# One written order for all units in place of a planner, in a linear-attention and expert-layer kernel

## The chip, the cores and the metric

The kernel runs on one core of one Trainium2 chip. A core has five engines that run side by side and wait for each other by semaphores: PE (matmuls and transposes; its weight loads are listed as PEld), DVE (elementwise work), ACT (functions of one argument, copies with a scale), POOL (here: small copies and the loads of expert weights) and SP (here: all other loads and stores). Each engine works through its own instructions strictly in the order in which the program wrote them. The metric is the device time of one execution in microseconds, as the median of several runs.

## The reference

```python
# attention, for each of 8 batches and 8 heads, 576 tokens, head size 64
phi  = where(x > 0, x, exp(x) - 1) + 1
kv   = einsum('bhsd,bhse->bhde', phi(k), v)    # 64 x 64 for each head
z    = sum over tokens of phi(k)
x    = (phi(q) @ kv) / (phi(q) @ z + 1e-6)      # -> 8 x 576 x 512
# expert layer: 8 experts, 512 -> 1024 -> 512, one expert for each token
logits = x @ w_gate;  local = sigmoid(x @ w_local)
e      = argmax(logits) where s == 0 or local < 0.5, else the expert of the token before
out    = softmax(logits)[e] * (relu(x @ w1[e]) @ w2[e])
```

With these inputs every token of a batch uses the expert of its first token. The kernel computes with one expert for each batch and counts tokens for which this doesn't hold; only where there is one does a second, general program run (it does not run here).

## The kernel before

**Units.** The work is cut into 803 units, each a handful of instructions on one engine (some are only placeholders for a landing). A unit is a call `op(name, engine, length, rank, needs, function, takes, gives)` (lines 721 to 887). With `a` the batch (0 to 7), `n = 2a + j` a half of its heads, `h` a half of its tokens, they are:

- loads on SP: Lk, Lv, Lq (576 KB each, for every n), the stores ST, and HOLD, which stands in front of the loads of n = 4 and later until the first expert weights have landed; there are 4 buffers for k, 2 for q, 3 for v;
- E and E2 on ACT (exp and relu of k or q, lines 359 and 365), P on DVE (their sum, lines 387 and 394), VC (v copied beside ones, line 406), CL (the clamp of the first two k, line 379);
- K on PE (phi(k) times v, line 415: 72 matmuls with 72 weight loads), KC on DVE (its copy, line 420);
- Q and QL on PE (transposes of phi(q), lines 426 and 440), QC and QLC on ACT (their copies, lines 432 and 446);
- N and NL on PE (phi(q) times kv, lines 467 and 486), D and DL on DVE (the division, lines 452 to 455);
- X and XL on PE (transposes of x, lines 501 and 513), XC and XLC on DVE (their copies, lines 506 and 517);
- R on PE (the logits, lines 528 and 534), RC, PK, BK on DVE (copy, choice of the expert and of a weight slot, bookkeeping; lines 539 to 572), W on POOL (the load of the expert's w1 and w2, left out where the expert is in a slot already; lines 586 to 598), CW on DVE (copy of a slot into the current weights, lines 608 and 612);
- S1, S2, S3 on DVE, ACT, DVE (softmax value of the expert, lines 622 to 643);
- H on PE (8 for each batch, x times w1, line 650), HC on ACT (relu, line 657), O0 and O on PE (5 outputs for each batch, lines 669 and 673), OC on ACT (times the softmax value, lines 683 and 685).

The expert part of batch a runs on PE as H a 0 to H a 7, O0 a, O a 0 to O a 4. Units of the attention of later batches are written between these. K, N and NL work on 64 x 64 tiles of the array, the others mostly on the whole array.

**Planner.** `in_order` (lines 25 to 156) plays a schedule: each engine is free at some time, each unit has a length, a rank and needs; at each event each free engine takes the ready unit with the lowest rank, waits for a soon-ready one of lower rank, and so on. Ranks are nudged by hand-kept numbers, one table for each batch (`LATER`, lines 216 to 225). For PE it counts instructions in blocks and lets a block arrive some time after the one before it was entered:

```python
            wait += max(0.0, have - at)
            new.append(max(at, have) + (par["fetch"] if now < par["busy"] else par["fetch2"]))
```

with `"block": 256, "count": 62, "fetch": 5.6, "fetch2": 3.6` and the number of PE instructions of a unit as `instr` gives it (lines 205 to 213). What leaves the planner is only the order; the waits at run time are semaphores between the instructions.

**PSUM.** There are four slots of two banks. A unit that takes a slot gets the one that is free the earliest in the plan; at most 2 are held by units of kind "a" (attention, logits) and 3 by units of kind "m" (H, O). A unit then waits for the unit that gave the slot back.

**Products of zeros.** `work(n)` (line 895) writes n matmuls of a tile of zeros (128 x 512) ahead of a unit, into a slot of their own that is held from FILL to FILLED: 21 ahead of QL 0, 8 ahead of K 0, 2 ahead of NL 0, 4 ahead of XL 0, 2 ahead of R 0 0.

Of the kernel before, what the change touches and what calls it, by code (L numbers as in the profile page):

```python
# [22 lines left out]


def in_order(ops, slots, cap, rings, par):

    near, patience, hop = par["near"], par["patience"], par["hop"]
    n = len(ops)
    at_ = {op[0]: i for i, op in enumerate(ops)}
    users = [[] for _ in ops]
    miss = [0] * n
    for i, op in enumerate(ops):
        miss[i] = len(op[4])
        for d in op[4]:
            users[at_[d]].append(i)
    engines = list(dict.fromkeys(op[1] for op in ops))  # L40
    free_at = {e: 0.0 for e in engines}
    ready = {e: [] for e in engines}
    due = [0.0] * n
    slot = [0.0] * len(slots)
    held = {c: 0 for c in cap}
    left = {r: [0.0] * k for r, k in rings.items()}
    got = {}
    begun, done, order = {}, {}, []
    for i in range(n):
        if not miss[i]:  # L50
            ready[ops[i][1]].append(i)
    last_q = False
    now, todo, later = 0.0, n, set()

    def place(kind, k):

        if held[kind] == cap[kind]:
            return None, None
        best = min(((max(slot[i], now), slots[i], i) for i in range(len(slots))
                    if slots[i] >= k and slot[i] is not None), default=None)  # L60
        return (None, None) if best is None else (best[2], slot[best[2]])

    block = par["block"]
    count, there = par["count"], [0.0, 0.0]

    def stalled(name, length):

        k, wait, t = par["instr"](name), 0.0, now
        b = (count - 1) // block
        new = []  # L70
        while (b + 1) * block < count + k:
            b += 1
            at = now + wait + length * (b * block - count) / k
            have = new[-1] if b >= len(there) else there[b]
            wait += max(0.0, have - at)
            new.append(max(at, have) + (par["fetch"] if now < par["busy"] else par["fetch2"]))
        return k, wait, new

    events = [0.0]
    while todo:  # L80
        if not events:
            raise AssertionError([ops[i][0] for e in engines for i in ready[e]][:20])
        now = heapq.heappop(events)
        while events and events[0] <= now:
            heapq.heappop(events)
        for e in engines:
            if free_at[e] > now:
                continue
            best, soon = None, []
            for i in ready[e]:  # L90
                name, _, length, rank, needs, takes, gives = ops[i]
                at, where = due[i], None
                if takes:
                    if takes[1]:
                        where, t = place(*takes)
                        if where is None:
                            continue
                    else:
                        if not left[takes[0]]:
                            continue  # L100
                        t = min(left[takes[0]])
                    at = max(at, t)
                if e == "PE":
                    if last_q and par["quarter"](name):
                        rank -= par["cont"]
                    if at <= now:
                        rank += par["stall"] * stalled(name, length)[1]
                if at > now:
                    heapq.heappush(events, at)
                    soon.append((rank, at))  # L110
                elif best is None or rank < best[0]:
                    best = (rank, i, where)
            if not best:
                continue
            rank, i, where = best
            name, _, length, _, needs, takes, gives = ops[i]
            if isinstance(length, tuple):
                length = length[free_at["WQ"] > now + 1]
            if any(r < rank - near and t < now + (0.9 if r < -60 else patience) * length for r, t in soon):
                continue  # L120
            if e == "PE":
                q = par["quarter"](name)
                if q and not last_q:
                    length = length + par["switch"]
                last_q = q
                k, wait, new = stalled(name, length)
                count += k
                there += new
                length += wait
            ready[e].remove(i)  # L130
            order.append(name)
            begun[name] = now
            end = free_at[e] = done[name] = now + length
            todo -= 1
            heapq.heappush(events, end)
            if takes:
                if takes[1]:
                    slot[where] = None
                    held[takes[0]] += 1
                    got[name] = where  # L140
                else:
                    left[takes[0]].remove(min(left[takes[0]]))
            if gives:
                t = ops[at_[gives]][5]
                if t[1]:
                    slot[got[gives]] = end + hop
                    held[t[0]] -= 1
                else:
                    left[t[0]].append(end + hop)
            for u in users[i]:  # L150
                miss[u] -= 1
                due[u] = max(due[u], end + (0.0 if ops[u][1] == e else hop))
                if not miss[u]:
                    ready[ops[u][1]].append(u)
                    heapq.heappush(events, due[u])
    return order, begun, done, got
# [3 lines left out]
def kernel(  # L160
# [12 lines left out]
    P = 128  # L173
    B, H, S, Dh = q.shape
# [9 lines left out]
    NJ = 2  # L184
# [11 lines left out]
    CAP = {"a": 2, "m": 3}  # L196

    def quarter(name):

        return name[0] in ("K", "N", "NL") or name[0] == "R" and name[2] == 0 or name[0] == "O" and name[2] == NC - 1  # L200


    fills = {("QL", 0): 21, ("K", 0): 8, ("NL", 0): 2, ("XL", 0): 4, ("R", 0, 0): 2}

    def instr(name):

        t = name[0]
        n = {"K": 8 * C * NJ, "N": 64, "NL": 32, "Q": 16, "QL": 4, "X": 16, "XL": 4, "H": 16, "O0": 14, "TOT": 4}.get(t, 0)
        if t == "R":
            n = 32 if name[2] else 16  # L210
        if t == "O":
            n = (2, 16, 16, 16, 32)[name[2]]
        return n + 2 * fills.get(name, 0)


    LATER = [
# [8 lines left out]
    ]  # L225

    PAR = {"near": 3.0, "patience": 0.2, "hop": 0.2, "cont": 20.0, "switch": 0.2, "quarter": quarter,
           "instr": instr, "block": 256, "count": 62, "fetch": 5.6, "fetch2": 3.6, "busy": 125, "stall": 10.0}

# [8 lines left out]
    with ExitStack() as main:  # L238
# [482 lines left out]
        def op(name, eng, length, rank, needs, fn, takes=None, gives=None):  # L721
            ops.append((name, eng, length, rank + later(name), [d for d in needs if d], takes, gives))
            run[name] = fn

        def later(name):

            kind = name[0]
            if kind == "lat":
                return 0
# [415 lines left out]
```

## Time and profile before

| | |
|---|---|
| median of 3 runs | 228.78 us (227.97 to 231.41) |
| the profiled execution | 228.7 us |
| its span, first to last instruction | 226.8 us |
| granted TensorE clock | 0.997 |
| busy PE / DVE / ACT | 208.7 / 153.9 / 155.3 us |
| first H on PE (H 0 0) | 26.87 us |
| first O0 on PE (O0 0) | 42.51 us |
| last matmul ends | 220.57 us |

The page gives busy time by engine and the chain of work that ended last. The view of waits names, for each wait, the engine and line that waited, then the one it waited for, the total in us, how often, and the longest. The timeline of an engine has the start and duration in us of a run of like instructions, and in brackets the idle time before it with what ended it. "issue" there is time in which the engine waited for nothing that the profile shows.

### The profile page before, as it was taken

The page shows a single profiled execution, that of the slowest core. Times are in us where ns is not written, and L with a number is a line of the kernel's source. Part 1 is how long each engine was busy: PE and PEld are TensorE (multiplying, and loading weights), DVE is VectorE, ACT ScalarE, POOL GpSimd, SP SyncE. Part 2 cuts the span into 40 slices and gives each one's busy share as a digit, 9 for nine tenths or more (in the row PEclk, how much of TensorE's full clock was granted, in tenths as well). Part 3 has the DMA queues.
Part 4 walks back from the last instruction along what each step waited for, and adds up shares of the span by engine and source line. Part 5 has one row for each costly group of instructions (what it writes and reads, how often), then busy time and mean ns, then how long its engine had stood idle before and what let it go on. Part 6 is the DMA issues. An engine that isn't in the chain of part 4 may idle for free.

```text
span 226.8 us, 8581 instructions
## 1 busy us (share of the span) xinstructions
PE 208.7 (92%) x3705; PEld 149.1 (66%) x3719; DVE 153.9 (68%) x428; ACT 155.3 (68%) x226; POOL 13.1 (6%) x41
## 2 busy tenths in 40 slices
PE   7996799799999999999987996999999999999990
PEld 2465688458876678865775584865887678648540
DVE  1868986798999896866949975793783857412300
ACT  3698877899999949697797765935736355546440
POOL 4004000010001000020000000110000003000000
PEclk9999999999999999999999999999999999999998
DMA  6999999585788698989992656089700018985032
GB/s 209 382 347 353 203 271 399 205 312 203 224 259 299 200 359 254 389 143 258 307 313 87 228 218 214 3 145 192 246 7 0 4 46 198 204 136 208 3 143 78
DMA packets 24142, 46.78 MB, mean 206 GB/s; under 512 B 2834, under 2 KB 8978, under 8 KB 23202
## 3 DMA queue, kind: packets, MB, share of 16 engines
q1 hardware_dynamic: 16914, 37.58, 46.8%
q0 software_dynamic: 6832, 8.45, 22.7%
q8 instruction: 31, 0.51, 0.9%
q10 hardware_dynamic: 352, 0.13, 0.2%
q14 instruction: 13, 0.11, 0.1%
HBM read 61.88 MB, written 9.44 MB: 314 GB/s over the span
## 4 chain that ended last, share of the span: by engine, by line
PE 52%; DMA 9%; DVE 9%; issue 3%; ACT 0%; DVEq 0%
PE yps L669 18%; PE hps L650 17%; DMA w2s<-in_moe_w_dram 9%; PE nps L467 4%; PE kvps L415 3%; PE tq L426 3%; PE yps L673 3%; PE tx L501 2%; DVE xb L455 2%; DVE fq L394 1%; DVE w2cur L612 1%; DVE xT L506 1%; PE lps L534 1%; DVE rec L454 1%; DVE w1cur L612 1%
## 5 line engine op out<-in xcount | busy, mean ns | idle before, releaser
L650 PE MATMUL hps<-xT,w1cur 128*128 128x288 bf16 x512 | 69.2, 286 | 2.6 <-issue 1.9
L657 ACT ACTIVATE hT<-hps 128x576 bf16<-128x576 f32 x64 | 41.3, 652 | 30.8 <-PE hps L650 30.8
L669 PE MATMUL yps<-w2cur,hT 128*128 128x512 bf16 x243 | 58.2, 379 | 2.5 <-DVE w2cur L612 1.8
L650 PEld LDWEIGHTS <-w1cur 128*128 128x128 bf16 x512 | 48.2, 98 | 15.2 <-issue 2.4
L669 PEld LDWEIGHTS <-hT 128*128 128x128 bf16 x256 | 24.3, 98 | 27.4 <-issue 2.0
L683 ACT ACTIVATE yo<-yps,pr 128x512 f32<-128x512 f32 x32 | 22.0, 690 | 22.3 <-PE yps L669 20.9
L455 DVE TENSOR_TENSOR xb<-nps,rec 128x512 bf16<-128x512 f32 x32 | 22.1, 691 | 1.1
L394 DVE SCALAR_TENSOR_TENSOR fq<-fq,qraw 128x576 f32<-128x576 f32 (+1 forms) x32 | 22.5, 739 | 0.0
L467 PE MATMUL nps<-kv,qT 64*64 64x65 f32 x1024 | 20.4, 221 | 2.3 <-ACT qT L432 2.1
L467 PEld LDWEIGHTS nps<-kv,qT 64*64 64x64 f32 x1024 | 17.4, 134 | 5.6 <-ACT qT L432 2.8
L359 ACT ACTIVATE ek<-kraw 128x1152 f32<-128x1152 f32 x16 | 18.5, 1158 | 3.3 <-DMA kraw<-in_k_dram 2.1
L432 ACT COPY qT<-tq 128x512 f32<-128x512 f32 x32 | 18.3, 639 | 2.0 <-PE tq L426 2.0
L415 PE MATMUL kvps<-vone,kraw 64*64 64x65 f32 x1152 | 19.6, 219 | 0.0
L359 ACT ACTIVATE fq<-qraw 128x1152 f32<-128x1152 f32 (+1 forms) x16 | 18.4, 1153 | 1.4 <-DMA qraw<-in_q_dram 1.4
L415 PEld LDWEIGHTS kvps<-vone,kraw 64*64 64x64 f32 x1152 | 18.1, 134 | 1.8 <-issue 0.4
L387 DVE SCALAR_TENSOR_TENSOR kraw<-ek,kraw 128x1152 f32<-128x1152 f32 x14 | 18.9, 1348 | 0.0
L365 ACT ACTIVATE qraw<-qraw 128x1152 f32<-128x1152 f32 (+1 forms) x16 | 18.4, 1151 | 0.3
L426 PE MATMUL tq<-ident,fq 128*128 128x128 f32 x128 | 16.9, 275 | 0.3 <-DVE lt_all L539 0.2
L365 ACT ACTIVATE kraw<-kraw 128x1152 f32<-128x1152 f32 x14 | 16.1, 1163 | 0.2
L426 PEld LDWEIGHTS tq<-ident,fq 128*128 128x128 f32 x128 | 14.2, 141 | 1.5 <-DVE lt_all L539 0.5
L612 DVE COPY w2cur<-w2s 128x4096 bf16 x7 | 8.5, 1220 | 7.7 <-PE yps L673 4.6
L506 DVE COPY xT<-tx 128x1024 bf16<-128x1024 bf16 x16 | 10.8, 683 | 3.4 <-PE tx L501 3.2
(93 smaller groups left out, 187.0 us busy)
## 6 DMA issues: line engine op xcount, KB each, us to landing
kraw<-in_k_dram SPq DMA_DIRECT2D x16, 576.0 KB, 8.1
vraw<-in_v_dram SPq DMA_DIRECT2D x16, 576.0 KB, 6.5
qraw<-in_q_dram SPq DMA_DIRECT2D x14, 576.0 KB, 5.9
w1s<-in_moe_w_dram POOLq DMA_DIRECT2D x7, 1024.0 KB, 9.3
w2s<-in_moe_w_dram POOLq DMA_DIRECT2D x7, 1024.0 KB, 17.3
out_dram<-yo SPq DMA_DIRECT2D x14, 512.0 KB, 4.9
qraw<-in_q_dram SPq DMA_DIRECT2D x2, 512.0 KB, 8.6
w1cur<-in_moe_w_dram POOLq DMA_DIRECT2D x2, 512.0 KB, 7.7
```

The source lines that it names most:

```text
L359: nc.scalar.activation(e[:, :, c0:c1, :], raw_, Act.Exp)
L365: nc.scalar.activation(raw_, raw_, Act.Relu)
L387: nc.vector.scalar_tensor_tensor(r, e, 1.0, r, Alu.min, Alu.add)
L394: nc.vector.scalar_tensor_tensor(e[:, g], e[:, g], 1.0, r[:, g], Alu.min, Alu.add)
L415: nc.tensor.matmul(ps[g * PH:(g + 1) * PH, t, :W], lhsT=f[h, g, c, :], rhs=vo[h, g, c, :], start=(c == 0), stop=(c == C - 1))
L426: nc.tensor.transpose(ps[:, r, i * P:(i + 1) * P], ex_[n, "q"][:, 1 + i + (NC - 1) * r, :, :], identity=ident)
L455: nc.vector.tensor_tensor(dst, ps[:, :, :, :Dh].rearrange("p g (i t) e -> p g i t e", t=2), rec.rearrange("p g (i t o) -> p g i t o", t=2, ...
L467: nc.tensor.matmul(ps[o * PH:(o + 1) * PH, g, (il * 2 + t) * W:(il * 2 + t + 1) * W], lhsT=qT[n][g * PH:(g + 1) * PH, t, i * P + o * PH:i ...
L650: nc.tensor.matmul(ps[:, u, :HS], lhsT=w1b[:, kk, m * P:(m + 1) * P], rhs=xT[b][:, kk, u * HS:(u + 1) * HS], start=(kk == 0), stop=(kk == ...
L657: nc.scalar.activation(hT[b][:, m, :].rearrange("p (u s) -> p u s", u=2), open_.pop(("H", b, m))[:, :, :HS], Act.Relu)
L669: nc.tensor.matmul(ps, lhsT=hT[b][:, m, i * P:(i + 1) * P], rhs=w2b[:, m, :], start=(m == 0), stop=(m == FK - 1))
L683: nc.scalar.activation(ym[:, i, :], ps, Act.Copy, scale=pr[:, i:i + 1])
```

## The change

The planner, its lengths, ranks and nudges are no longer used. A table `TURNS` holds 803 numbers: the units, by their place in the list of `op` calls, in the order in which they are written. `in_order` walks this table, asserts that the needs of a unit have been written before it, and hands out PSUM slots: a unit gets the slot that was given back the longest ago in written order. There is no limit by kind any more. The needs have one more member (OC waits for the OC before it), and the length of K is another, which nothing reads.

```diff
-def in_order(ops, slots, cap, rings, par):
...
+def in_order(ops, slots, rings, turns):
...
+    assert sorted(turns) == list(range(len(ops)))
+    took = {op[0]: op[2] for op in ops}
+    free, left = list(range(len(slots))), dict(rings)
+    got, order, seen = {}, [], set()
+    for i in turns:
+        name, needs, takes, gives = ops[i]
+        assert all(d in seen for d in needs), name
+        if takes and takes[1]:
+            got[name] = next(s for s in free if slots[s] >= takes[1])
+            free.remove(got[name])
+        elif takes:
+            left[takes[0]] -= 1
+            assert left[takes[0]] >= 0, name
+        if gives and took[gives][1]:
+            free.append(got[gives])
+        elif gives:
+            left[took[gives][0]] += 1
+        seen.add(name)
+        order.append(name)
+    return order, got
...
-    CAP = {"a": 2, "m": 3}
...
-    fills = {("QL", 0): 21, ("K", 0): 8, ("NL", 0): 2, ("XL", 0): 4, ("R", 0, 0): 2}
...
-    LATER = [
...
+    fills = {("FILL",): 19, ("QL", 0): 2, ("NL", 0): 2, ("XL", 0): 4, ("R", 0, 0): 2}
...
+    TURNS = [
+        8, 801, 0, 25, 3, 28, 5, 9, 1, 15, 2, 7, 30, 16, 11, 12, 4, 6, 10, 47, 29, 31, 26, 37, 38, 27, 798, 104,
...
-                op(("K", n), "PE", 1.1, r - head, [("P", "k", n), ("VC", n)],
+                op(("K", n), "PE", 1.2, r - head, [("P", "k", n), ("VC", n)],
...
-                op(("OC", a, i), "ACT", 0.62, a * NU + FK + i - 14, [("O", a, i), ("S3", a)],
+                op(("OC", a, i), "ACT", 0.62, a * NU + FK + i - 14, [("O", a, i), i and ("OC", a, i - 1), ("S3", a)],
...
-        order, begun, done, where = in_order(ops, SLOTS, CAP, {"ek": NK}, PAR)
+        order, where = in_order(ops, SLOTS, {"ek": NK}, TURNS)
```

Read back into names, the two orders differ as follows where the prediction speaks of them. The products of zeros are 29 in place of 37.

- DVE from the choice of the first expert to the first x. Before: P q 1 (first half), RC 0 0, PK 0, P q 1 (second half), BK 0, P k 2, D 0 0 0, VC 2, D 0 0 1, D 0 1 0, D 0 1 1, VC 3, XC 0 0, XC 0 1. Changed: P q 1 (first half), XLC 0, P q 1 (second half), RC 0 0, PK 0, VC 2, D 0 0 0, BK 0, D 0 0 1, D 0 1 0, P k 2, VC 3, D 0 1 1, XC 0 0, KC 2, XC 0 1.
- PE from H 0 2 to O0 0. Before: H 0 2, QL 1, H 0 3, Q 3, H 0 4, N 1 0 0, K 3, H 0 5, NL 1, N 1 1 0, N 1 1 1, XL 1, H 0 6, X 1 0, R 1 0, H 0 7, O0 0. Changed: H 0 2, QL 1, Q 2, Q 3, H 0 3, K 3, N 1 0 1, NL 1, N 1 1 1, H 0 4, XL 1, N 1 0 0, R 1 0, H 0 5, H 0 6, X 1 1, H 0 7, N 1 1 0, O0 0.
- ACT in the same stretch. Before: HC 0 1, S2 0, HC 0 2. Changed: HC 0 2, QLC 1, QC 2, S2 0, QC 3.
- PE around H 4 0. Before: O 3 4, K 10, K 13, N 5 0 0, NL 5, H 4 0, H 4 1. Changed: O 3 4, N 6 0 1, H 4 0, H 4 1, H 4 2, QL 7, K 15, NL 6, Q 14, R 4 1, XL 6, Q 15, X 6 1, NL 7, N 7 0 1, N 7 1 0, X 6 0, H 4 3.
- The attention as a whole is written earlier: the last X on PE (X 7 1) stands behind H 6 4 before, and behind O 4 4 in the change. From there on PE has only H, O, three R and one small sum. Between H 0 0 and H 2 0 the change writes 2 Q, 1 QL and 2 N more on PE, 2 E, 2 E2, 2 QC and 1 QLC more on ACT, and 2 D, 1 DL, 1 KC and 1 P more on DVE.
- The choice of batch 3's expert (R 3 0 on PE) stands behind H 2 2 before and behind H 2 1 in the change; between it and O0 3 there are 29.5 us of PE work before and 37.5 us in the change, counted by the durations of the units.

More of the change, by code (lines that the diff above doesn't have):

```diff
@@ L19 @@
 PSUM = bass.MemoryType.PSUM
-import heapq
-def in_order(ops, slots, cap, rings, par):
[L31 to L156, printed above, removed]
@@ L721, in op @@
         def op(name, eng, length, rank, needs, fn, takes=None, gives=None):
-            ops.append((name, eng, length, rank + later(name), [d for d in needs if d], takes, gives))
+            ops.append((name, [d for d in needs if d], takes, gives))
             run[name] = fn
[L725 to L729, printed above, removed]
-            if kind in ("E", "E2", "P"):
-                kind += name[1]
-            elif kind in ("X", "XC", "R", "RC", "O", "OC", "H", "HC"):
-                kind += str(name[2])
-            elif kind in ("N", "D"):
-                kind += f"{name[2]}{name[3]}"
-            elif kind in ("Q", "K", "QC", "KC", "VC"):
-                kind += str(name[1] % NJ)
-            more = LATER[batch]
-            return more.get(kind, 0) + (0 if kind[0] in "HO" or kind in ("CW", "WL") else more.get("", 0))
         NU = FK + NC
@@ L887 @@
         op(("FILLED",), "PE", 0.0, -999, [("X", 0, 1)], lambda: None, gives=("FILL",))
-        size = {o[0]: o[5][1] for o in ops if o[5]}
-        order, begun, done, where = in_order(ops, SLOTS, CAP, {"ek": NK}, PAR)
+        size = {o[0]: o[2][1] for o in ops if o[2]}
+        order, where = in_order(ops, SLOTS, {"ek": NK}, TURNS)
         got.update(where)
```

12 lines of the change are left out of this document (removed), and 45 rows, old and new, of tables (LATER, TURNS).

## The prediction

> **What bounds the kernel now.** The page comes first: how full is each engine?
>
> ```profile
> span 226.8 us, 8581 instructions
> ...
> PE 208.7 (92%) x3705; PEld 149.1 (66%) x3719; DVE 153.9 (68%) x428; ACT 155.3 (68%) x226; POOL 13.1 (6%) x41
> ```
>
> PE is the bound, and the change leaves its products alone but for 8 of zeros. A new order can only take away PE's idle time, 226.8 - 208.7 = 18.1 us. The view of PE's waits, with PE's timeline beside it, says what that is made of.
>
> ```profile
> PE nps L467 <- ACT qT L432: 2.1, 2, 1.5
> PE hps L650 <- issue: 1.9, 1, 1.9
> PE yps L669 <- DVE w2cur L612: 1.8, 1, 1.8
> PE fill L897 <- DVE warm L284: 1.3, 1, 1.3
> PE lps L528 <- issue: 1.2, 1, 1.2
> PE tx L501 <- DVE xb L455: 1.2, 2, 0.8
> PE hps L650 <- ACT yl L685: 0.5, 1, 0.5
> PE tq L426 <- DVE lt_all L539: 0.2, 1, 0.2
> ...
> PE hps L650 <- DVE lt_all L539: 0.2, 1, 0.2
> PE tq L426 <- DVE kv L420: 0.2, 1, 0.2
> ```
>
> ```profile
> 26.87 1.14 PE L650 MATMUL hps<-xT,w1cur 128*128 128x288 bf16 x8
> ...
> 39.83 0.29 PE L528 MATMUL lps<-wg,xT 128*64 128x9 bf16 x4
> 41.32 0.26 PE L528 MATMUL lps<-wg,xT 128*64 128x9 bf16 x4 [1.20 <-issue]
> ...
> 42.51 0.81 PE L669 MATMUL yps<-w2cur,hT 128*128 128x512 bf16 x2
> ```
>
> ```profile
> 131.65 2.33 PE L415 MATMUL kvps<-vone,kraw 64*64 64x65 f32 x144
> 133.80 0.65 PE L467 MATMUL nps<-kv,qT 64*64 64x65 f32 x32
> 134.27 0.42 PE L486 MATMUL npl<-kv,qT 64*64 64x65 f32 x16
> 134.61 2.01 PE L650 MATMUL hps<-xT,w1cur 128*128 128x288 bf16 x15
> 138.54 0.30 PE L650 MATMUL hps<-xT,w1cur 128*128 128x288 bf16 x1 [1.92 <-issue]
> ```
>
> ```profile
> 219.51 1.06 PE L673 MATMUL yps<-w2cur,hT 128*64 128x256 bf16 x16
> ```
>
> Three stages. **The front**, up to H 0 0 at 26.87, where loads, DVE and ACT lead and PE waits about 5 us besides the zeros (2.1, 1.3, 1.2 and small ones). **The middle**, from there to 220.57 (219.51 + 1.06), where PE leads and loses 1.2 + 1.9 + 1.8 + 0.5 + 3 x 0.2 = 6.0 us. **The tail** of 226.8 - 220.6 = 6.2 us: the last output and its store, whose order stays. So the middle has at most 6.0 us to give, and the front only what moves H 0 0.
>
> The two "issue" gaps fall in the middle of a unit (after 4 of 8, after 15 of 16 matmuls), where no data can be missing. Ahead of each stands the densest run of small matmuls: before the second, 144 + 32 + 16 + 15 matmuls, each with a weight load, 414 instructions in 5.0 us. Counted as the kernel's own `instr` counts (blocks of 256, 62 ahead of the first), a block ends in R 1 0 and, to some ten instructions, in H 4 1. The queue that moves instructions fits:
>
> ```profile
> q8 instruction: 31, 0.51, 0.9%
> ```
>
> 0.51 MB in 31 packets is 16 KB each, and PE's 3705 + 3719 instructions make 29 blocks of 256. So I read these gaps as waits for PE's own code. By my count the block that ended at 41.3 was entered at 35.3, and the one that ended at 138.5 at 132.9: the next one took 6.0 and 5.6 us to be there. Two other blocks (K 5 to K 4, then to XL 2, around 52 to 62) were used up in 4.6 and 4.8 us without a gap, so it is sometimes there sooner.
>
> **The change part by part.** I counted the table's order by unit, with the durations of before.
>
> Fewer zeros (PE's and DVE's timeline):
>
> ```profile
> 8.89 1.89 PE L897 MATMUL fill<-zero 128*128 128x512 bf16 x8
> ...
> 10.58 0.75 DVE L406 COPY vone<-vraw 128x1152 f32<-128x1152 f32 x1
> ```
>
> Nothing. The 8 ahead of K 0 fill PE while DVE copies the second v, for which K 1 waits; and SP now issues that load behind 512 KB of q (Lq 0 before Lv 1), which uses up what the zeros free. The bounds are the 1.9 us that they took, either way.
>
> The front. DVE leads to H 0 0, so its timeline is the one to read,
>
> ```profile
> 17.31 0.67 DVE L394 SCALAR_TENSOR_TENSOR fq<-fq,qraw 128x512 f32<-128x512 f32 x1
> 17.91 1.34 DVE L387 SCALAR_TENSOR_TENSOR kraw<-ek,kraw 128x1152 f32<-128x1152 f32 x1
> 19.51 0.17 DVE L452 TENSOR_SCALAR den<-nps 128x8 f32<-128x8 f32 x1 [0.26 <-PE nps L467]
> ...
> 20.55 0.75 DVE L406 COPY vone<-vraw 128x1152 f32<-128x1152 f32 x1
> ...
> 25.21 1.28 DVE L506 COPY xT<-tx 128x1024 bf16<-128x1024 bf16 x2
> ```
>
> and the tile vraw, asked for the third and fourth load alone:
>
> ```profile
> L256 SPq DMA_DIRECT2D vraw<-in_v_dram x2: 1171/1172/1174, 9.6 to 10.8; - x2
> ...
> DMA to landing us min/median/max: 9.5/9.6/9.7
> ```
>
> Now VC 2 is written ahead of D 0 0 0, and the third v lands at 9.6 + 9.5 = 19.1. PK 0, done by 17.31 before, ends near 17.7, with half of P q 1 and XLC 0 in another place ahead of it; then DVE idles 1.4 us, where before it did P k 2. From 19.1: VC 2 0.7, three D of 1.04 (19.51 to 20.55), P k 2 1.3, VC 3 0.7, another D, two XC of 0.64 and KC 2, some 0.2, between them: 27.4. H 0 0 began 0.4 after the second XC (25.21 + 1.28 = 26.5), so it starts at **27.8, 0.9 later**. The first expert's weights had landed by 26.87, where H 0 0 reads them; with PK 0 some 0.4 later that is 27.3 at most, so this load isn't last.
>
> H 0 0 to O0 0: one N more, which is missing later (no change in sum). S2 0 is now behind QC 2 on ACT, so S3 0, CW 0 0 and KC 3 come later on DVE; behind KC 3 wait D 1 0 1, DL 1, D 1 1 1, XLC 1, and for the last R 1 0 on PE: **+0.5** (0 to 1.5).
>
> Later waits. The 1.8 is the load of batch 3's w2, as the chain of work shows in order of time:
>
> ```profile
> 97.33 21.40 DMA w2s<-in_moe_w_dram
> ...
> 118.83 1.24 DVE w2cur L612
> ```
>
> It lands 0.1 us ahead of the copy that holds O0 3. R 3 0, which starts its choice, stands 37.5 us of PE work ahead of O0 3 in place of 29.5; a load of the same 21.4 us is 8 us early. So **-1.8**. The 0.5 and the three 0.2 are single slot waits; with slots by age I find no unit whose slot is given back late, counting each engine's work between a PE unit and the PE unit that waits for it: **-1.1**. They may come back elsewhere (0 to 3 us).
>
> Code waits. Both old places go: **-1.2 and -1.9**. The attention is packed closer while its loads run, and blocks are used up faster (K 1.1, N 0.5, H 1.0 us, as in the rows above, Q 0.9): 3.9 us (Q 2 to NL 1), 4.2 (K 4 to Q 4), and twice 4.7 (to N 4 1 0, to N 4 1 1). Before had four such blocks, and paid 1.2, 1.9, 0, 0: 0.8 each. So **+3.1**, from 0 to 1.9 each, and more if blocks of 5 us count too. I take the mean, since the four of before are the nearest rows there are. Two more of 4.8 and 4.5 come near H 4 2, with the loads done; I give them nothing.
>
> The sum, on the profiled execution's 228.7: -4.8 (the gaps after 42.5) - 1.2 + 0.9 + 0.5 + 3.1 = -1.5, so **227.2**. That execution lies at the median (228.78).
>
> The Trainium skill, page "Runtime: NRT & Kernel Launch", section "Instruction fetch mechanics", says that blocks of 16 KiB (256 instructions) are refilled by the sequencer's own DMA queue and that crossing one costs a tail bump, "mostly hidden". The 16 KB agree with the queue's row; "hidden" would leave no gaps of 1.2 and 1.9.
>
> **The rivals.**
>
> *Code is there in time.* If the next block takes less than 3.9 us, as for the two blocks near 60 it nearly did, the +3.1 is nothing: **224.1**. Against it: two gaps of before. The skill's section above, taken at its word, is this rival. If H 0 0 isn't late either, 223.2.
>
> *Code is late everywhere (the other side).* If the next block takes 5.7 us each time, as at the two gaps, every block used faster pays: 3.9, 4.2, 4.5, 4.7, 4.7, 4.8, 5.0, 5.2, 5.2, 5.3, 5.3, 5.5 pay 10.1 us together: 228.7 - 6.0 + 1.4 + 10.1 = **234.2**. For it: more loads are in flight between 45 and 120 us, and blocks are fetched beside them. From 5.2 us a block (4.6 us in sum) the change loses.
>
> *ACT becomes the bound* from H 0 0 to H 2 0.
>
> ```profile
> 26.87:83.40 56.53, 54.73 (x1141) 40.63 (x1142) 49.77 (x126) 48.30 (x69) 2.10 (x7) 1.00 0.83 268
> 50.00:60.00 10.00, 9.72 (x289) 7.97 (x288) 9.33 (x21) 9.70 (x14) 0.00 (x0) 1.00 0.56 199
> ...
> 70.00:80.00 10.00, 9.89 (x213) 6.20 (x214) 9.09 (x19) 9.78 (x12) 0.70 (x2) 1.00 0.76 243
> ```
>
> ```profile
> L359 ACT ACTIVATE ek<-kraw 128x1152 f32<-128x1152 f32 x16 | 18.5, 1158 | 3.3 <-DMA kraw<-in_k_dram 2.1
> ...
> L432 ACT COPY qT<-tq 128x512 f32<-128x512 f32 x32 | 18.3, 639 | 2.0 <-PE tq L426 2.0
> ...
> L426 PE MATMUL tq<-ident,fq 128*128 128x128 f32 x128 | 16.9, 275 | 0.3 <-DVE lt_all L539 0.2
> ```
>
> Columns of the first: stretch, length, then busy PE, PEld, DVE, ACT. The change adds 2 E and 2 E2 of 1.16, 2 QC of 1.14 (18.3 by 16) and a QLC of some 0.4: 7.3 us on ACT's 48.3 there. PE gets 2 Q of 0.9 to 1.06 (16.9 by 16), 2 N of 0.47 (133.80 to 134.27) and a QL of 0.2, some 3.0 us on 56.5. So ACT has 55.6 of 59.5, 93%. Before ran at 97% with PE fed (50 to 60, 70 to 80). If ACT must idle as before (8.2 us) it needs 63.8, 4.3 more: **231.5**.
>
> *The order does nothing*: each wait only moves. 228.7.
>
> **How the numbers follow.** Forecast 227.2: 0.50. Code in time, 224.1: 0.25. Code late everywhere, 234.2: 0.12. ACT, 231.5: 0.08. Nothing, 228.7: 0.05. A measurement of this kernel tells about 2% (4.6 us) from no change: faster means under 224.2, slower over 233.4. Half of the rival at 224.1 and a little of the forecast's low end are faster: 0.20. Slower is the late-code case with a little of ACT: 0.13. The range is 222.8 (code in time, H 0 0 on time, and no front wait) to 232.0, which holds the forecast, the first rival and most of ACT's.
>
> **What would show it.** H 0 0 at 27.8, with DVE waiting ahead of VC 2 for the third v; no wait of line 669 for line 612; "issue" gaps on PE inside units near NL 1 (36 us), Q 4 (52), and N 4 1 0 and N 4 1 1 (90 to 110), near 3 us together; ACT 93% busy up to H 2 0; the last X on PE some 20 us earlier than before. It is wrong if PE's waits in the middle name ACT, DVE or a load of k, q or v for over 3 us, or if the "issue" gaps are none or over 6 us.

## The result and the profile after

The changed kernel takes 237.93 us (median of 4 runs, 237.25 to 239.09), the kernel before 229.09 beside it: a ratio of 1.041 (95% interval 1.034 to 1.047), slower by some 9 us. The forecast was 227.2, with 232.0 as its upper end. The profiled execution took 237.83 us, 9.13 more than that of before (228.7). Ratios here and below leave disturbed executions out, while a median stands over all of a kernel's runs.

Four rows of the page of the changed kernel: span, busy time by engine, the granted clock in 40 slices (6 us each), and the queue that moves instructions.

```profile
span 236.1 us, 8582 instructions
...
PE 211.3 (89%) x3699; PEld 150.8 (64%) x3711; DVE 152.6 (65%) x428; ACT 155.5 (66%) x226; POOL 13.7 (6%) x41
...
PEclk9979999999999999999999979999999999999998
...
q8 instruction: 31, 0.51, 0.8%
```

PE is still the bound, and its code is as long as before (31 packets). Its idle time has grown, and two slices have a 7 in place of the 9 of the others. The view of PE's waits (engine, line, what it waited for, us in total, times, longest):

```profile
PE hps L552 <- issue: 6.0, 4, 2.6
PE tq L328 <- issue: 2.1, 1, 2.1
PE fill L784 <- DVE warm L186: 1.3, 1, 1.3
PE nps L369 <- DVE den L354: 1.2, 2, 0.9
PE kvps L317 <- DVE vone L308: 1.2, 1, 1.2
PE yps L575 <- issue: 1.1, 1, 1.1
PE tx L403 <- issue: 0.9, 1, 0.9
PE nps L369 <- issue: 0.8, 1, 0.8
```

The wait for w2cur is no longer among them, nor the slot waits of before. "issue" has 10.0 us behind H 0 0 (6.0 + 2.1 + 1.1 + 0.8; the 0.9 of tx is ahead of it), where before had 3.1; the timeline adds two of 0.2 (one of them is put down to ACT there). To place the time, the middle as one stretch, first of the changed kernel, then of before (length, then busy PE, PEld, DVE, ACT, POOL, clock, DMA share, GB/s):

```profile
28.46:230.35 201.89, 190.36 (x3257) 137.14 (x3264) 133.52 (x383) 134.87 (x202) 8.97 (x21) 0.99 0.65 188
134.90:138.30 3.40, 3.40 (x16) 2.17 (x15) 2.10 (x7) 1.20 (x3) 0.17 (x1) 0.50 0.01 2
```

```profile
26.87:220.57 193.70, 186.84 (x3255) 135.52 (x3264) 134.84 (x384) 134.59 (x202) 8.36 (x21) 1.00 0.68 197
```

The 9.1 us are: H 0 0 at 28.46 instead of 26.87, +1.6; PE's idle time in the middle, 201.89 - 190.36 = 11.5 instead of 6.9, +4.7 (the code waits, 10.0 against 3.1, are +6.9; all other waits, the two of 0.2 among them, -2.3, rounded); PE busy for 190.36 instead of 186.84 with the same products, +3.5; the tail and what lies around the span, -0.6. The second row above has part of the +3.5: for 3.40 us the granted clock was 0.50. PE's timeline shows it beginning behind the longest gap, and an earlier such stretch in the front, where 72 products of K 1 take 2.23 us and the same 72 of K 0 took 1.28:

```profile
9.72 1.28 PE L317 MATMUL kvps<-vone,kraw 64*64 64x65 f32 x72 [0.81 <-ACT vone L306]
12.16 2.23 PE L317 MATMUL kvps<-vone,kraw 64*64 64x65 f32 x72 [1.16 <-DVE vone L308]
...
133.64 5.63 PE L552 MATMUL hps<-xT,w1cur 128*128 128x288 bf16 x31 [2.64 <-issue]
```

Where do the issue gaps lie? The view by stretches, cut just ahead of each gap, counts the instructions between one and the next (PE's and PEld's, in brackets):

```profile
36.90:56.65 19.75, 19.06 (x382) 13.00 (x382) 17.67 (x46) 17.03 (x21) 0.57 (x3) 1.00 0.77 279
56.65:69.00 12.35, 11.48 (x254) 9.64 (x254) 11.58 (x30) 11.51 (x18) 0.00 (x0) 1.00 0.79 270
69.00:75.30 6.30, 4.15 (x127) 3.41 (x128) 4.88 (x19) 5.17 (x8) 0.00 (x0) 1.00 1.02 403
75.30:105.60 30.30, 28.86 (x633) 22.39 (x635) 26.00 (x69) 27.51 (x38) 3.06 (x5) 1.00 0.73 234
105.60:121.50 15.90, 14.72 (x252) 9.81 (x253) 12.76 (x35) 12.56 (x20) 0.00 (x0) 1.00 1.12 267
121.50:133.50 12.00, 9.38 (x255) 7.87 (x256) 10.17 (x28) 9.28 (x11) 0.22 (x2) 1.00 0.71 261
133.50:160.30 26.80, 26.48 (x508) 19.17 (x510) 18.64 (x51) 12.93 (x23) 2.59 (x4) 0.94 0.28 63
```

Matmuls and weight loads together: 764, 508, 255, 1268, 505, 511, 1018. These are 3, 2, 1, 5, 2, 2 and 4 blocks of 256, less a few matmul records that the trace lacks and PE's semaphore instructions (with a few others of its sequencer), which these columns leave out. Counted with those from the start of the program, 193 or 194 instructions more than a multiple of 256 stand ahead of the first weight load behind each of these gaps. The same holds in every trace of this document: they have 64 idle times of PE of 0.4 us or more that the view calls "issue", and all 64 lie there. Every issue gap of the middle thus lies at the end of a block of PE's instructions, whatever unit stands there: N, H, Q, O. Below, "block gap" means such a gap.

The traces also hold the packets of queue q8, 16 KB each, and so show the wait itself. A block is entered where the count above says so; times are in us, and the last column is PE's idle time at the end of that block:

| kernel | block entered | packet begins | packet lands | PE goes on to the next block | idle |
|---|---|---|---|---|---|
| changed | 69.10 | 73.04 | 74.00 | 75.39 | 2.14 |
| changed | 127.86 | 131.35 | 132.31 | 133.64 | 2.64 |
| changed | 53.02 | 54.17 | 55.15 | 56.74 | 0.16 |
| before | 132.75 | 136.20 | 137.16 | 138.54 | 1.92 |
| before | 57.31 | 59.30 | 60.26 | 61.77 | none |

Of the 64 gaps, 63 end 1.2 to 1.5 us behind the landing of such a packet. The packet takes about 1 us in each row; what differs is how long after the entry it begins.

### The profile page after: what moved, and what is told of

It reads as the page before. It is cut to its first block, busy times and chain, and to the rows that moved or that the text cites. A ratio compares the mean times of both kernels' runs of the same rounds, so it can differ in the third digit from the quotient of the medians.

```text
span 236.1 us, 8582 instructions
## 1 busy us (share of the span) xinstructions
PE 211.3 (89%) x3699; PEld 150.8 (64%) x3711; DVE 152.6 (65%) x428; ACT 155.5 (66%) x226; POOL 13.7 (6%) x41
## 3 DMA queue, kind: packets, MB, share of 16 engines
q0 software_dynamic: 6832, 8.45, 22.1%
## 4 chain that ended last, share of the span: by engine, by line
PE 77%; DVE 8%; issue 6%; DMA 5%; SPq 1%; ACT 0%
PE hps L552 25%; PE yps L571 23%; PE kvps L317 6%; PE nps L369 6%; PE tq L328 6%; DMA vraw<-in_v_dram 5%; PE yps L575 3%; PE tx L403 2%; DVE xb L357 2%; PE lps L436 1%; DVE kraw L289 1%; DVE xT L408 1%; SPq L158 1%; DVE vone L308 1%; PE npl L388 1%
## 5 line engine op out<-in xcount | busy, mean ns | idle before, releaser
L552 PEld LDWEIGHTS <-w1cur 128*128 128x128 bf16 x512 | 49.1, 99 | 20.7 <-issue 7.6
L571 PE MATMUL yps<-w2cur,hT 128*128 128x512 bf16 x245 | 57.1, 379 | 0.6
L585 ACT ACTIVATE yo<-yps,pr 128x512 f32<-128x512 f32 x32 | 21.3, 686 | 21.6 <-PE yps L571 21.5
L369 PE MATMUL nps<-kv,qT 64*64 64x65 f32 x1024 | 21.4, 222 | 2.1 <-DVE den L354 1.2
L317 PE MATMUL kvps<-vone,kraw 64*64 64x65 f32 x1152 | 21.2, 226 | 2.0 <-DVE vone L308 1.2
L357 DVE TENSOR_TENSOR xb<-nps,rec 128x512 bf16<-128x512 f32 x32 | 22.1, 691 | 1.2
L334 ACT COPY qT<-tq 128x512 f32<-128x512 f32 x32 | 18.3, 638 | 6.0 <-PE tq L328 5.9
L317 PEld LDWEIGHTS kvps<-vone,kraw 64*64 64x64 f32 x1152 | 19.2, 140 | 4.5 <-issue 1.7
L369 PEld LDWEIGHTS nps<-kv,qT 64*64 64x64 f32 x1024 | 18.0, 134 | 5.2 <-issue 2.4
L261 ACT ACTIVATE fq<-qraw 128x1152 f32<-128x1152 f32 (+1 forms) x16 | 18.3, 1146 | 1.2 <-DMA qraw<-in_q_dram 1.2
```

The lines of the kernel that those rows point to most:

```text
L261: nc.scalar.activation(e[:, :, c0:c1, :], raw_, Act.Exp)
L317: nc.tensor.matmul(ps[g * PH:(g + 1) * PH, t, :W], lhsT=f[h, g, c, :], rhs=vo[h, g, c, :], start=(c == 0), stop=(c == C - 1))
L357: nc.vector.tensor_tensor(dst, ps[:, :, :, :Dh].rearrange("p g (i t) e -> p g i t e", t=2), rec.rearrange("p g (i t o) -> p g i t o", t=2, ...
L369: nc.tensor.matmul(ps[o * PH:(o + 1) * PH, g, (il * 2 + t) * W:(il * 2 + t + 1) * W], lhsT=qT[n][g * PH:(g + 1) * PH, t, i * P + o * PH:i ...
L552: nc.tensor.matmul(ps[:, u, :HS], lhsT=w1b[:, kk, m * P:(m + 1) * P], rhs=xT[b][:, kk, u * HS:(u + 1) * HS], start=(kk == 0), stop=(kk == ...
L571: nc.tensor.matmul(ps, lhsT=hT[b][:, m, i * P:(i + 1) * P], rhs=w2b[:, m, :], start=(m == 0), stop=(m == FK - 1))
```

## Experiments

The theory: the time went into waits for blocks of code, which depend on where a block's end falls among the units and on the loads that run then; the clock's loss follows from PE's idle time. The rivals: the zeros, the slots by age, or operands that are late at fixed places of the written order.

**The zeros moved, not changed in number** (changed kernel):

```diff
-    fills = {("FILL",): 19, ("QL", 0): 2, ("NL", 0): 2, ("XL", 0): 4, ("R", 0, 0): 2}
+    fills = {("FILL",): 11, ("QL", 0): 2, ("K", 0): 8, ("NL", 0): 2, ("XL", 0): 4, ("R", 0, 0): 2}
```

> The changed kernel with as many zeros as it has (29 products), 8 of them moved from its start to their old place ahead of K 0; the numbers of PE's instructions from NL 0 on stay the same. Theory (the clock is gated down between 12.0 and 15.4 because PE idles 0.8 and 1.2 us ahead of K 0 and K 1): no clock event in the front, the second half of K takes 1.2 in place of 2.2 us, H 0 0 at about 27.0 in place of 28.5, some 1.5 us less in all (236.4). Rival (H 0 0 is late because DVE waits for the third v ahead of VC 2, as the prediction had it): H 0 0 stays within 0.4 of 28.5 and the time at 237.9.

Measured: 240.09 us (236.5 to 241.12), ratio 1.047 (1.041 to 1.054). A miss: the half clock in the front only came earlier (9.5 to 13.0), H 0 0 stayed at 28.48, and the gaps stayed at the same instructions. This says little on the zeros. One row of its timeline is of use, the same 31 products of H behind nearly the same gap as in the changed kernel:

```profile
133.76 3.96 PE L552 MATMUL hps<-xT,w1cur 128*128 128x288 bf16 x31 [2.56 <-issue]
```

Here the clock stayed full: 3.96 us instead of 5.63. A half-clock stretch costs 1.7 us, and a gap of this length doesn't always bring one.

**Loads of an eighth**, in both kernels (of k, q and v from the third batch on). The kernels leave out seven eighths of each such load, the tile keeps older numbers there, and with other numbers fewer expert weights are loaded as well:

```diff
+            rows_ = P if n < LEAD * NJ else P // 8
             ap = bass.AP(src.tensor, (b * H + j * (H // NJ)) * S * Dh + c0 * Dh,
-                         [[run, P], [P * run, 2], [1, (c1 - c0) * Dh]])
+                         [[run, rows_], [P * run, 2], [1, (c1 - c0) * Dh]])
+            dst = dst[:rows_]
```

> The changed kernel with an eighth of each load of k, q and v from n = 4 on (16 of 128 partitions; the rest of each tile keeps older numbers, so the outputs are others and fewer expert weights are loaded). Order, waits and instruction numbers are unchanged. Theory (PE's 'issue' gaps are waits for its own code, whose fetch stands behind the loads in the DMA queues): the gaps after H 0 0, 10.4 us in all, fall under 3 us, the gated clock at 134 goes, and the time falls to 226 to 229. Rival (a fetch takes its 5 us whatever the queues do): the gaps stay near 10 us and the time above 235. Rival (the gaps are hidden waits for loaded data): they go as well, but then they need not sit at every 256th instruction.

> The kernel before with the same eighth of the loads: the partner of the run of the changed kernel. Theory: its two gaps (3.1 us) and the wait for w2 (1.8 us) go, about 223 to 224. If the changed order is the better one once code is in time, its partner run lies below this one; by the prediction's sum by about 3 us less what the front costs.

Measured: 225.81 us (changed order) and 224.52 us (old order), one execution each, so there is no interval for the 1.3 us between them. The middle of the first, then of the second, by the view by stretches:

```profile
29.04:218.20 189.16, 188.13 (x3268) 136.72 (x3264) 133.20 (x383) 133.97 (x201) 4.83 (x21) 1.00 0.29 79
```

```profile
28.22:216.82 188.60, 186.74 (x3268) 135.53 (x3264) 133.97 (x384) 134.27 (x202) 5.35 (x21) 1.00 0.29 80
```

With a DMA share of 0.29 instead of 0.65, the changed order's idle time in the middle falls from 11.5 to 1.0 us (189.16 - 188.13), 0.6 of it at one block's end: code is hardly late when the queues are quiet. Its order, slots and instructions are the same as in the change, so none of them makes those waits by itself. And what is left shows the order alone: it has 0.8 us less idle time than the old one and 1.4 us more busy time, at full clock in both. Even with code nearly in time the changed order isn't ahead in this pair.

**The old order, its blocks moved by 64 instructions**: 53 products of 203 columns in place of the first 21 of 512, about the same time of zeros.

```diff
+                if n == 21:
+                    for _ in range(53):
+                        nc.tensor.matmul(fill[:, :203], lhsT=zero[:, :P], rhs=zero[:, :203], start=True, stop=True)
+                    return
                 for _ in range(n):
```

> The kernel before with 53 products of 203 columns of zeros in place of 21 of 512 at its start: the same columns in all, 64 PE instructions more, so that every block of 256 ends 64 instructions earlier in the work. Nothing else moves. Theory (gaps are code waits and their place is set by where blocks end): the gaps at 41.3 and 138.5 go or move to other units, all of them at instruction numbers that are 64 less by 256 in the order's own count, and the sum changes; counted with 5.3 us for a fetch, from 5 to some 19 us: slower by 5 to 15 us. Rival (the gaps belong to the units in which they fall, as waits for data or slots): the same two gaps at R 1 0 and H 4 1, the time within 1 us of 229.

Measured: 241.68 us (238.73 to 245.21), ratio 1.045 (1.036 to 1.054). Its waits, and the count between two of them:

```profile
PE nps L467 <- issue: 4.8, 2, 2.4
PE npl L486 <- issue: 4.6, 2, 3.2
PE lps L534 <- issue: 2.4, 2, 1.4
```

```profile
115.30:146.70 31.40, 27.40 (x510) 19.81 (x510) 22.77 (x58) 22.68 (x33) 0.59 (x4) 1.00 0.74 226
```

510 + 510 is four blocks again. None of these products waited for code in the kernel before. Moving the blocks, with order and slots untouched, costs the old kernel as much as the whole change does.

**The parts of the change alone**, each on the kernel before: its zeros, and its slots by age.

```diff
-                work(fills.get(name, 0))
+                work({("FILL",): 19, ("QL", 0): 2, ("NL", 0): 2, ("XL", 0): 4, ("R", 0, 0): 2}.get(name, 0))
```

```diff
+        kinds = {o[0]: (o[5], o[6]) for o in ops}
+        free_, where = list(range(len(SLOTS))), {}
+        for nm in order:
+            takes, gives = kinds[nm]
+            if takes and takes[1]:
+                where[nm] = free_.pop(0)
+            if gives and kinds[gives][0][1]:
+                free_.append(where[gives])
         got.update(where)
```

> The kernel before with the zeros of the change alone: the 8 products of zeros ahead of K 0 are left out, the order of all units and the PSUM slots are those of before. The blocks of TensorE's instruction stream end 16 instructions (8 products, each with its weight load) further along in the units. Theory of code blocks and clock: the front loses what the change's front lost (H 0 0 at about 28.5 instead of 26.9, with some 3.4 us of granted clock at half after TensorE's idle time ahead of K 0), the middle keeps few code waits (2 to 4 us of gaps, at other units than 41.3 and 138.5): 229 to 231.5, of which the whole is the front. Rival, the zeros themselves make the change slow: 236 to 239. Rival, they cost nothing, as forecast: 228 to 229.

> The kernel before with the PSUM slots given out by age alone: the order of all units and the zeros are those of before. No instruction is added or taken away, so the blocks end at the same instructions. Theory of code blocks and clock: same within 1%, 227 to 231, the gaps of TensorE at 41.3 and 138.5 again at the same instruction and of a like size. Rival, the slots' order makes the small-tile units wait or be slower: the middle longer by 3 us or more without a larger gap, 232 or above.

Measured: zeros 229.75 us, ratio 1.004 (0.999 to 1.008); slots 230.73 us, ratio 1.004 (0.999 to 1.008). Neither is a measurable part of the 4.1%. What is left is the written order, with the block ends that it brings.

**Eight zeros put back ahead of K 0 in the changed kernel**:

```diff
+    fills = {("FILL",): 19, ("QL", 0): 2, ("K", 0): 8, ("NL", 0): 2, ("XL", 0): 4, ("R", 0, 0): 2}
```

> The changed kernel with 8 products of zeros put back ahead of K 0 (37 in all, the written order unchanged). Blocks of TensorE's instruction stream end 16 instructions earlier in the units. Theory of code blocks and clock: no half clock in the first 20 us, H 0 0 at about 27 as before (1.4 us earlier than in the changed kernel), and the code waits of the middle stay, at other units, 9 to 13 us in sum: 235 to 239, with every gap at the same place modulo 256 instructions. Rival, the 8 zeros are the cause: 229 to 231. Rival, fixed places in the written order (a missing operand at 75, 134 and 166 us): the gaps stay ahead of the same products.

Measured: 241.12 us (236.93 to 243.5), ratio 1.040 (1.031 to 1.049). The rival (8 zeros missing) falls. In the profiled execution (243.5 us) the front was not as expected: no half clock in the first 20 us, but one at 24.0 to 27.4 behind a block gap of 1.45, and H 0 0 at 29.28.

**Twenty-nine zeros at the old places**, old order:

```diff
-                work(fills.get(name, 0))
+                work({("QL", 0): 19, ("K", 0): 6, ("NL", 0): 1, ("XL", 0): 2, ("R", 0, 0): 1}.get(name, 0))
```

> The kernel before with 29 products of zeros at the old places (19 ahead of QL 0, 6 ahead of K 0, 1, 2 and 1 ahead of NL 0, XL 0, R 0 0), order and slots unchanged. Up to R 0 0 the stream has 16 instructions fewer, so the blocks end 16 instructions further along. Theory of code blocks: the two gaps at 41.3 and 138.5 (3.1 us in sum) move and shrink to 2 us or less, the front keeps its clock (8 zeros fewer, but 6 of them still ahead of K 0): 226.5 to 228.5. Rival, alignment does not matter: 228.5 to 229.5. Rival, every zero counts for the clock: half clock in the front, 230 to 232.

Measured: 229.93 us, ratio 1.002 (0.998 to 1.005): a miss. In its profile the two block gaps did shrink (none of 0.15 or more is left near 41.3, and 0.35 of the other), but the clock was at half from 18.3 to 25.1 and H 0 0 came at 28.71.

**Float32 zeros**, to move blocks without cooling PE. `zero` becomes a float32 tile of 448 (changed order), 160 or 400 columns (old order):

```diff
-    fills = {("FILL",): 19, ("QL", 0): 2, ("NL", 0): 2, ("XL", 0): 4, ("R", 0, 0): 2}
+    fills = {("FILL",): 6, ("K", 0): 2, ("NL", 0): 1, ("XL", 0): 1, ("R", 0, 0): 1}
...
-        zero = consts.tile([P, 512], BF16, name="zero")
+        zero = consts.tile([P, 448], F32, name="zero")
...
-                    nc.tensor.matmul(fill, lhsT=zero[:, :P], rhs=zero, start=True, stop=True)
+                    nc.tensor.matmul(fill[:, :448], lhsT=zero[:, :P], rhs=zero, start=True, stop=True)
```

> The changed kernel, written order and slots untouched, with other zeros: 11 products of 448 float32 columns (6 at the start, 2 ahead of K 0, 1 each ahead of NL 0, XL 0, R 0 0) in place of 29 of 512 bf16 columns. By the time that a float32 product of 64x65 takes beside a bf16 one they stream about as long as 38 of the old ones, with 36 instructions fewer (22 for 58), so every block of TensorE's instruction stream ends 36 instructions further along in the units. Theory of code blocks: the gaps of the middle, 10.4 us in the changed kernel, halve (4 to 7), still all at the same place modulo 256; with the clock kept in the front the time is 229.5 to 233.5. Rival, the changed order itself waits at fixed units: gaps at the same products as in the changed kernel, 236 to 239. Rival, the loss is the clock in the front alone: 236.

> The kernel before, order and slots untouched, with 28 products of 160 float32 columns (16 ahead of QL 0, 6 ahead of K 0, 1, 3 and 2 ahead of NL 0, XL 0, R 0 0) in place of 37 of 512 bf16 columns: the same streaming time by estimate, 18 instructions fewer. Theory of code blocks: the two gaps at 41.3 and 138.5 (3.1 us) shrink to under 1.5 in sum as with 29 zeros, and the front keeps its clock: 226 to 228. Rival, no gain: 228.5 to 230.

Measured: 237.49 us, ratio 1.033 (1.028 to 1.038), and 238.56 us, ratio 1.035 (1.029 to 1.042). Both missed, for one reason. The groups by line of the old order's run show it:

```profile
L898 PE MATMUL fill<-zero 128*128 128x160 f32 x56 | 10.6, 348 | 1.2 <-DVE warm L285 1.2
```

28 products are written and 56 run, with 56 weight loads: such a float32 product is two. K of the kernel before shows the same (36 written, 72 run), while the float32 transposes of Q run once. So the blocks moved by 11 x 4 - 58 = -14 and 28 x 4 - 74 = +38 instructions, not by -36 and -18. Read that way they are two more points: the old order at +38 is as slow as the change. Its waits have the block gaps in npl and hps:

```profile
PE npl L487 <- issue: 4.0, 2, 2.1
PE hps L651 <- issue: 2.2, 1, 2.2
```

**The changed order moved by half a block**: 83 products of 117 columns for the first 19.

```diff
+                if n == 19:
+                    for _ in range(83):
+                        nc.tensor.matmul(fill[:, :117], lhsT=zero[:, :P], rhs=zero[:, :117], start=True, stop=True)
+                    return
```

> The changed kernel with 83 products of zeros of 117 columns in place of 19 of 512 at its start: about the same streaming time, 128 instructions more, so blocks end half a block earlier in the units. Theory of code blocks: as many us of gaps (8 to 13 in the middle) as in the changed kernel, but none of them at the products where it had them, all at the same place modulo 256: 236 to 242. Rival, fixed units of the written order: gaps at the same products as in the changed kernel.

Measured: 245.56 us (two runs), ratio 1.070 (1.063 to 1.077), more than expected. Its waits:

```profile
PE nps L369 <- issue: 10.0, 4, 4.1
PE kvps L317 <- issue: 3.4, 3, 1.8
```

hps, tq and yps, which had 9.2 of the 10.0 us in the changed kernel, have none. So the order has no fixed places at which something is late.

**The changed order moved by -30**, where an estimate from the distances between its block ends had its least:

```diff
+    fills = {("FILL",): 5, ("K", 0): 1, ("XL", 0): 1}
```

> The changed kernel, written order and slots untouched, with 7 float32 products of 448 columns of zeros (5 at the start, 1 ahead of K 0, 1 ahead of XL 0). The last two runs showed that such a product of 128 rows is two products with a weight load each, 4 instructions, so this is 28 instructions for 58: blocks end 30 instructions further along, where the model made from the distances of the block ends has its least (half of what it has for the changed kernel). Theory of code blocks: gaps of the middle 4 to 7 us instead of 10.4, 231 to 235. Rival, the changed order costs about 10 us of code waits wherever its blocks end: gaps of the middle 9 to 12, 236 to 240.

Measured: 232.84 us (230.05 to 236.74), ratio 1.013 (1.009 to 1.017), inside the range expected. The waits (the profiled execution took 233.92):

```profile
PE nps L369 <- issue: 1.9, 2, 1.1
...
PE npl L388 <- issue: 1.3, 1, 1.3
PE hps L552 <- DVE w2cur L514: 1.2, 1, 1.2
```

With 1.9 of txl, 0.8 of a tq put down to ACT and one of 0.1 they come to some 7.2 us. The third row is a block gap too: it lies at a block's end, 1.4 us behind a packet of code, and hps reads xT and w1cur, never w2cur; the name is that of the last event seen. The written order is that of the change, instruction for instruction behind the zeros; only the block ends lie elsewhere, and two thirds of the loss are gone (from 4.1% to 1.3%).

**The old order moved by -18**:

```diff
+    emit = {("QL", 0): 7, ("K", 0): 3, ("NL", 0): 1, ("XL", 0): 2, ("R", 0, 0): 1}
```

> The kernel before, order and slots untouched, with 14 float32 products of 400 columns of zeros (7 ahead of QL 0, 3 ahead of K 0, 1, 2 and 1 ahead of NL 0, XL 0, R 0 0): 56 instructions for 74, so blocks end 18 instructions further along, with about the same streaming time. Theory of code blocks: gaps of the middle at the block ends under 1.5 us in sum instead of 3.1, 226 to 228.5. Rival, its gaps there have nothing to gain: 228.5 to 231.

Measured: 231.34 us, ratio 1.004 (0.999 to 1.008). The gain didn't come: the gap at 138.5 shrank, but another block, at 39.75, had one.

```profile
PE kvps L416 <- issue: 2.4, 1, 2.4
```

So the distance between block ends tells a bad place from a good one, but not among the good ones. No version with all of the loads is faster than the kernel before.

## Why the prediction was wrong

**The step that failed is "Code waits", by its size.** What was late was named rightly, and that the two old gaps would go and others come. The sum put +3.1 in place of the old 3.1, so nothing in all; it measured 10.0 in place of 3.1, +6.9, and 10.0 is beyond the 6 us that the prediction had named as a sign that it is wrong. It took four blocks, used in 3.9 to 4.7 us, at 0.8 each. Cut at their ends, the changed kernel's blocks behind H 0 0 that paid were nine: used in 3.1, 3.5, 4.0, 4.2, 4.8, 4.8 and 4.9 us, they paid 2.6, 0.2, 1.3, 2.1, 0.8, 1.1 and 1.2; two of 5.5 and 6.0 us paid 0.9 and 0.2. So both the count and the price were low. Use and wait together are 5.3 to 6.4 us in eight of the nine (in the stretch from 69.00 to 75.30 above they are one whole block), as at the two gaps of before (6.0 and 5.6 by the prediction's count); the ninth, at 56.7, has 3.7. That is the rival "code is late everywhere", which took 5.7 us for each block, came to 10.1 in sum and was given 0.12. The 0.8 was a mean over four blocks of before, two of which paid nothing.

Shown: the waits stand behind the loads (gone with small loads), at block ends only, each ends just behind a packet of code, and they move with the block ends. But the time of use alone doesn't set the price, in the prediction's sum or in that rival's. Counted with the semaphore instructions, the kernel before has seven blocks behind H 0 0 that are used in 3.9 to 5.1 us. For the two that paid, the packet of the next block began 3.6 and 3.5 us after the entry; for the other five, 0.4 to 2.0. In the changed kernel it began after 2.9 to 4.0 us for eight of the nine, and after 1.2 for the ninth. In the kernel before the DMA share over the block goes with it (1.05 and 0.92 for the two, 0.03 to 0.76 for the five); in the changed kernel not each time (0.65 for the block that paid 2.6). What a late packet stands behind wasn't tried.

**That rival's 234.2 is still 3.7 short.** The prediction says that "A new order can only take away PE's idle time": it put PE's busy time at no change, and in the middle it grew by 3.5. The clock wasn't in any sum. The 3.4 us at half behind the gap at 133.64 cost 1.7 (5.63 against 3.96), so a code wait can be paid more than once. Of the +3.5 of busy time in the middle 1.8 is left, and the pair with small loads has 1.4 of it with the clock full and hardly a wait for code: the changed order's products themselves take longer. Its small products (K, N, NL, on 64x64 tiles) are entered from other units more often, 27 times against 19 by my count of the two orders behind H 0 0; that this is the cause wasn't tested and stays open.

**The front**: H 0 0 at 28.46, forecast 27.8. The reason given, a wait for the third v, isn't what this trace shows. DVE's timeline, first of the changed kernel, then of it with eight zeros back ahead of K 0:

```profile
19.52 0.14 DVE L451 COPY tag<-e0f 1x1 f32<-1x1 f32 x1
19.59 0.74 DVE L308 COPY vone<-vraw 128x1152 f32<-128x1152 f32 x1
```

```profile
19.26 0.76 DVE L308 COPY vone<-vraw 128x1152 f32<-128x1152 f32 x1 [0.65 <-DMA vraw<-in_v_dram]
```

In the first, VC 2 follows the choice of the expert with no wait for the third v. It was the choice that was late (PK 0 was to end near 17.7), behind K 1 at half clock. From VC 2 to H 0 0 are 8.9 us, and the prediction had 8.7 for that chain. In the second, where K 1 runs at full clock, the choice is early enough and VC 2 does wait for the third v, until 19.26 (forecast 19.1). So the mechanism was there, hidden behind a later one.

**Zeros, "nothing"**: right alone (ratio 1.004), within the bounds given. In the old order, the profile of before has no half clock up to its last matmul, and in the two runs with 29 zeros H 0 0 came at 28.7. That the zeros keep the clock up isn't shown: the old order with small loads has all 37, a half clock from 18.7 to 22.1, and H 0 0 at 28.22.

**Later waits, -1.8 and -1.1**: right. No yps waits for w2cur, and all waits that aren't code fell by 2.3 (2.6 with the two of 0.2 counted as code). **S2 0, +0.5**: 0.3, within its bounds.

**ACT as the bound**: no. Up to H 2 0 (which starts at 90.9) ACT is busy 52.58 of 62.44 us, 84%; forecast were 55.6 of 59.5, 93%. The stage is longer than forecast, and ACT had less to do in it:

```profile
28.46:90.90 62.44, 57.72 (x1223) 43.57 (x1222) 53.21 (x136) 52.58 (x76) 2.43 (x7) 1.00 0.82 270
```

**Is the crossing of a block hidden?** The Trainium skill, page "Runtime: NRT & Kernel Launch", section "Instruction fetch mechanics", calls the crossing of a block "mostly hidden". With small loads this case agrees (1.0 us idle in all); with its real loads it doesn't (10.0 us).

## What to carry to other kernels

Where a kernel is one long unrolled stream and PE is the bound, count its instructions in blocks of 256 and mark the ends: an "issue" gap in the middle of a unit is a block that came late. Its price here was what the block before it lacked, in time of use, to some 5.3 to 6.4 us where the packet of code began late, beside full queues; where it began early, blocks used in 4.5 us paid nothing. An order found at one alignment of the blocks has that alignment built in, so compare two orders over a few shifts of the stream (some products of zeros more or fewer at the start) before one of them is called better. And price a wait of PE with the clock that may follow it.

## What was not expected of the hardware

- The same program with its code moved by 64 instructions is 4.5% slower, and by 38 instructions 3.5%, with nothing else than zeros changed. Of one order the ratios to the kernel before run from 1.013 (moved by -30) over 1.041 (not moved) to 1.070 (by +128).
- Half clock follows waits shorter than its own length: 3.4 us at half behind 2.64 us idle, and in the front behind 0.81 and 1.16 us with 1.28 us of work between. It is not certain, as 2.56 us without it shows. The record of the clock in the traces tells the two apart: within each trace all of its changes lie whole multiples of 3.413 us from each other, so time is cut into stretches of that length. Up to the last matmul, half clock followed each of the 13 stretches of full clock in which PE was idle for 2.05 us or more, 11 of the 23 with 1.59 to 2.03, and none of those with less. The gap of 2.64 put 2.17 us into one stretch (131.47 to 134.88); that of 2.56 was cut at 132.43 into 1.23 and 1.33. The Trainium skill, page "TensorE: Matmul & The Clock Gate", section "What's actually happening", has the clock fall after an idle window of about 3.4 us; the length of the slow stretch agrees (3.40), the idle time that brings it was shorter here.
